# Ranks zero and one of a mixture of experts leave by 32-wide turns on VectorE, rank one gets a narrow arm, and two late ranks hold 248 and 240 tokens

## The chip, the core and the metric

One NeuronCore of one Trainium2 chip runs the whole program in one launch. The metric is the device time of that launch in microseconds (us), the median of three runs. Beside it stands one profiled execution, from which every duration below is read.

## What is computed

The input is attention data (8 batches, 8 heads, 576 positions, 64 wide). Two attentions are added: one over means of four positions, spread back, and one over a band of seven neighbours. The result, laid out as 4608 tokens of 512 numbers, goes through a two-level mixture of 4 x 4 experts, and that part is what the change touches:

```python
g_idx = argmax(x @ w_group); e_idx = argmax(x[g] @ w_expert[g])   # one of 16 experts a token
h = np.maximum(xg[mask_e] @ w1[g, e], 0.0)        # 512 -> 1024
ye = h @ w2[g, e]                                 # 1024 -> 512
out[tok_idx] = (g_w * e_w)[:, None] * ye          # the token's own two softmax weights
```

All is float32. With the reference's own inputs (its routing, evaluated on them) one expert, with 329 tokens, is taken early; the other fifteen have 385, 366, 360, 312, 305, 300, 281, 265, 261, 260, 258, 246, 237, 233 and 210 tokens.

## The kernel before, in words

The attention comes first, with one expert (256 of its tokens early, the rest late) worked in beside its end. The other fifteen experts follow in order of size as ranks 0 to 14. An order written out by hand covers the attention; `begin` is a written list of steps that finishes the early expert and prepares rank 0; `main` then emits `ranked` for ranks 0 to 13, and `last_rank` does rank 14. Each engine executes its own instructions strictly in the order in which they were emitted.

A rank has a fixed width, `CAPS[r]`, in tokens. Each product of a pair of float32 operands is three TensorE matmuls (high by high, high by low, low by high). `hidden` makes one of eight 128-row blocks of h: 12 matmuls as wide as the rank. `project` adds one block into the result: 12 matmuls as wide as the rank (four 128-row parts of the result, tokens along the columns), or, where the width is a multiple of 128, three matmuls of 512 columns for each 128 tokens (tokens along the rows; "rows" in the code). So ranks 1, 13 and 14 (384, 256, 256) were projected by rows before.

`ranked` runs ten steps f. At f = 0 it drains the previous rank's result out of PSUM, GpSimd fetches the tokens of the rank after next by indirect DMAs, and from f = 2 on `project(f - 2)` writes the same PSUM banks again. Within the ten steps VectorE and ScalarE also split the next weights into high and low, and prepare the next rank's tokens.

A result leaves in one of three ways. Ranks 2 to 12 (`TURNED`): VectorE turns 32 x 32 blocks straight out of PSUM (`drain`), and GpSimd scatters 32 tokens at a time in quarter rows (`store_quarters`, up to 13 scatters); the columns of `w2` are permuted on the host for this (`w2q`), and the tokens' weights are multiplied in on the way in (`scale`, ScalarE, 128 x 512 for each 128 tokens). Rank 0: two copies on ScalarE and two on VectorE out of PSUM, then for each 128 tokens four TensorE transposes, a multiplication by the weight on ScalarE or VectorE (`store`) and one scatter of whole rows. Rank 1, 13, 14, by rows: `store` alone.

The tokens of ranks 0 and 1 are turned by TensorE on their way in (`turn_in`), those of later ranks by a DMA to and from DRAM (`lay_down`, `pick_up`) and VectorE.

Ranks in `SWITCHED` (0 and 3 to 12) exist twice, once at full width and once narrower by `LESS` = 20. A word of bits, computed from the counts, decides by a branch on every engine; the narrow arm is the one jumped to. TensorE gets a prefetch hint for the branch at f = 2 of the rank before. All eleven branches took the narrow arm here.

Seven steps of `begin`, in their order (late is the early expert's rest, st is rank 0):

```python
(self.weights_split, st, 0, "w2", V),
(self.weights_in, st, e, 2),
(self.project, late, 2),
(self.project, late, 3),
(self.turn_in, st, 0),
(self.turn_in, st, 1),
(self.turn_hidden, late, 3),
```

## Time and profile before

| | |
|---|---|
| three runs | 682.92, 684.72, 686.47 us; median 684.72 us |
| the profiled execution | 685.44 us; its span in the trace 683.7 us |
| TensorE matmul busy | 642.7 us (94% of the span) |
| VectorE, ScalarE, GpSimd busy | 489.3, 384.5, 353.7 us |
| DMA | 160.77 MB, mean 235 GB/s |

"Busy" counts the time in which at least one instruction of the engine runs. Matmuls overlap and their ends are modelled, so the distance between their starts says more than their durations. Lines such as L979 are lines of the kernel before: L979 and L995 hidden, L1028 and L1030 project (by rows, by columns), L964 `turn_in`, L1058 the transposes of `store`, L931 `scale`, L1041 `drain` by turns, L1072 the scatters, L1178 the branches, L886 the high half of a weight split, L957 that of tokens.

### The profile page before, as it was taken

How to read it: one execution, taken by the hardware profiler on the slowest of the kernel's cores; microseconds unless marked ns; L12 is line 12 of the kernel's file. 1: busy time of each engine (PE TensorE's matmuls, PEld its weight loads, DVE VectorE, ACT ScalarE, POOL GpSimd, SP SyncE). 2: the span in 40 equal slices, each digit the busy share in tenths (PEclk: the TensorE clock that was granted, in tenths of full speed). 3: DMA queues.
4: the chain of work that ended last, by engine and by line, in shares of the span. 5: the costliest groups of instructions: out<-in, count | busy, mean ns of one | idle time of the engine just before them, and what ended most of it. 6: DMA issues, size and time to landing. Idle time of an engine off the chain costs nothing. (4 is left out here: it accounts for less than half of the span.)

```text
span 683.7 us, 17694 instructions
## 1 busy us (share of the span) xinstructions
PE 642.7 (94%) x6743; PEld 573.8 (84%) x6743; DVE 489.3 (72%) x942; ACT 384.5 (56%) x833; POOL 353.7 (52%) x394
## 2 busy tenths in 40 slices
PE   7788997998987899999999999999999999999996
PEld 3565776676765788999899999999999999999995
DVE  5987988988896587644646667776776776777751
ACT  8776765775764536645544446456456456456531
POOL 7957556667542553403240446557547556455521
PEclk9999999999999999999999999999999999999999
DMA  8788899889778618959786778989999989999920
GB/s 305 207 253 264 270 295 269 272 230 263 238 207 263 201 29 265 319 166 247 222 218 203 206 217 235 250 264 280 234 271 277 253 250 273 270 271 268 284 70 27
DMA packets 128080, 160.77 MB, mean 235 GB/s; under 512 B 25445, under 2 KB 92783, under 8 KB 127968
## 3 DMA queue, kind: packets, MB, share of 16 engines
q1 hardware_dynamic: 102496, 129.99, 65.7%
q0 software_dynamic: 7952, 20.47, 10.1%
q10 hardware_dynamic: 17520, 8.85, 4.8%
q8 instruction: 66, 1.08, 0.7%
q14 instruction: 46, 0.38, 0.2%
HBM read 129.48 MB, written 31.03 MB: 235 GB/s over the span
## 5 line engine op out<-in xcount | busy, mean ns | idle before, releaser
L1072 POOL DMA_INDIRECT out_dram<-yt,qo x110 | 130.2, 1184 | 133.2 <-DVE qo L831 107.9
L983 ACT ACTIVATE hh<-ph 128x256 fp32r<-128x256 f32 (+13 forms) x128 | 53.3, 418 | 185.9 <-PE ph L979 184.0
L979 PE MATMUL ph<-xh,w1h 128*128 128x256 f32 (+13 forms) x512 | 153.8, 301 | 2.9 <-issue 2.8
L979 PE MATMUL ph<-xh,w1l 128*128 128x256 f32 (+13 forms) x512 | 153.0, 299 | 0.5 <-issue 0.5
L979 PE MATMUL ph<-xl,w1h 128*128 128x256 f32 (+13 forms) x512 | 153.1, 299 | 0.0
L984 DVE SCALAR_TENSOR_TENSOR hl<-ph,hh 128x256 fp32r<-128x256 f32 (+13 forms) x128 | 59.1, 464 | 86.4 <-ACT hh L983 86.0
L1030 PE MATMUL y<-hh,w2h 128*128 128x396 f32 (+11 forms) x384 | 115.9, 302 | 0.0
L1030 PE MATMUL y<-hh,w2l 128*128 128x396 f32 (+11 forms) x384 | 115.2, 300 | 0.5 <-issue 0.5
L1030 PE MATMUL y<-hl,w2h 128*128 128x396 f32 (+11 forms) x384 | 115.2, 300 | 0.0
L979 PEld LDWEIGHTS ph<-xh,w1h 128*128 128x128 f32 x512 | 96.6, 189 | 4.9 <-issue 4.0
L979 PEld LDWEIGHTS ph<-xl,w1h 128*128 128x128 f32 x512 | 96.7, 189 | 0.9
L979 PEld LDWEIGHTS ph<-xh,w1l 128*128 128x128 f32 x512 | 96.6, 189 | 0.1
L887 DVE TENSOR_TENSOR w2l<-raww,w2h 128x1024 fp32r<-128x1024 f32 x61 | 74.6, 1223 | 26.8 <-ACT w2h L886 24.8
L887 DVE TENSOR_TENSOR w1l<-raww,w1h 128x1024 fp32r<-128x1024 f32 x61 | 74.6, 1224 | 23.4 <-ACT w1h L886 22.6
L914 POOL DMA_INDIRECT xg<-xd,gi x47 | 53.2, 1132 | 54.9 <-ACT share L927 25.9
L1030 PEld LDWEIGHTS y<-hh,w2h 128*128 128x128 f32 x384 | 72.3, 188 | 1.3 <-ACT w2h L886 0.7
L1030 PEld LDWEIGHTS y<-hh,w2l 128*128 128x128 f32 x384 | 72.3, 188 | 0.7 <-issue 0.7
L1030 PEld LDWEIGHTS y<-hl,w2h 128*128 128x128 f32 x384 | 72.3, 188 | 0.0
L886 ACT ACTIVATE w1h<-raww 128x1024 fp32r<-128x1024 f32 x64 | 67.3, 1053 | 6.1 <-PE phr L995 2.7
L886 ACT ACTIVATE w2h<-raww 128x1024 fp32r<-128x1024 f32 x64 | 67.1, 1050 | 1.0 <-DMA raww<-in_moe_w_dram 1.0
L1072 POOL DMA_INDIRECT out_dram<-yo,oi x14 | 15.9, 1134 | 53.5 <-ACT yo L1063 20.6
L452 PE MATMUL b_x<-vw,pt 126*32 126x128 f32 x1152 | 38.0, 275 | 3.9 <-DMA vw<-odd 2.4
(247 smaller groups left out, 1268.3 us busy)
## 6 DMA issues: line engine op xcount, KB each, us to landing
raww<-in_w1q_dram SPq DMA_DIRECT2D x52, 512.0 KB
raww<-in_w2q_dram SPq DMA_DIRECT2D x44, 512.0 KB
raww<-in_moe_w_dram SPq DMA_DIRECT2D x32, 512.0 KB
vw<-in_vw_dram SPq DMA_DIRECT2D x32, 378.0 KB
kt<-in_k_dram SPq DMA_DIRECT2D x16, 576.0 KB
qT<-in_q_dram SPq DMA_DIRECT2D x16, 576.0 KB
xd<-x ACTq DMA_DIRECT2D x15, 576.0 KB
vs<-in_vm_dram SPq DMA_DIRECT2D x16, 512.0 KB
```

Source lines behind the costliest of these rows:

```text
L452: self.nc.tensor.matmul(pt[32 * j : 32 * j + 32, t], self.of("pt", u)[:ROWS, 32 * lin : 32 * lin + 32], self.windows(u)[:ROWS, :, lin], st ...
L886: self.nc.scalar.activation(hi, raw, AF.Copy)
L887: eng.tensor_tensor(out=lo, in0=raw, in1=hi.bitcast(F32), op=ALU.subtract)
L914: self.nc.gpsimd.indirect_dma_start(out=xg[:w], out_offset=None, in_=self.xd[0:rows], in_offset=bass.IndirectOffsetOnAxis(ap=st["gi"][:w, ...
L979: nc.tensor.matmul(ph, a[:, k, cs], st[b][:, k, 0:C], start=(n == 0), stop=(n == 11))
L983: nc.scalar.activation(hh, ph, AF.Relu)
L984: nc.vector.scalar_tensor_tensor(out=hl, in0=ph, scalar=0.0, in1=hh.bitcast(F32), op0=ALU.max, op1=ALU.subtract)
L1030: nc.tensor.matmul(y, a[:, f % 2, cs], b, start=(f == 0 and n == 0), stop=(f == 7 and n == 2))
L1072: i = self.nc.gpsimd.indirect_dma_start(out=out, out_offset=bass.IndirectOffsetOnAxis(ap=index, axis=0), in_=y, in_offset=None, bounds_che ...
```

## The change

Rank 0 and rank 1 join `TURNED`: their results leave by VectorE's turns and quarter scatters, their `w2` is read permuted, and their tokens are scaled on the way in, rank 0's by four steps in `begin` ahead of `turn_in`, rank 1's at f = 2, 3, 4 of rank 0 (rank 2's then at 4, 5, 6, and its `lay_down` at 7). Rank 1 joins `SWITCHED` with arms of 384 and 368 columns, and is projected by columns. Ranks 13 and 14 get 248 and 240 columns; they stay by rows. The lists of quarter rows have four columns for 13 ranks, the quarter's number is added when they are made, and the matrix they are made with lies in a result buffer. The copies, the transposes in `store`, and `keep_shares` for ranks go. Cut to its core:

```diff
-CAPS = [416, 384, 368, 352, 336, 320, 312, 304, 296, 288, 280, 272, 264, 256, 256, 384]
-LESS = 20
-SWITCHED = (0, *range(3, 13))
-TURNED = range(2, 13)
+CAPS = [416, 384, 368, 352, 336, 320, 312, 304, 296, 288, 280, 272, 264, 248, 240, 384]
+LESS = [16 if r == 1 else 20 for r in range(16)]
+SWITCHED = (0, 1, *range(3, 13))
+TURNED = range(13)
-SCALED = {3: (0,), 4: (1,), 5: (2,)}
...
     def quarter_lists(self, c):
-        pt = self.psum([P, hi - lo, 3], "ql")
...
-        self.nc.vector.tensor_copy(self.qf[:, c], pt)
+        pt = self.psum([P, hi - lo, 4], "ql")
...
+        self.nc.vector.tensor_scalar(out=self.qf[:, c], in0=pt, scalar1=self.quad, scalar2=None, op0=ALU.add)
...
+        self.four = self.yt[1][:, 0 : 4 * P].rearrange("p (c q i) -> p c q i", c=4, q=4)
...
     def drain(self, st):
-        for d in range(4):
-            if d % 2:
-                nc.vector.tensor_copy(yt[:, d], st["y"][d])
-            else:
-                nc.scalar.activation(yt[:, d], st["y"][d], AF.Copy)
+        nb = (st["C"] + 31) // 32
+        yt = st["yt"] = self.yt[st["r"] % 2][:, 0 : P * nb].rearrange("p (b d j) -> p b d j", d=4, j=32)
         for d in range(4):
+            self.nc.vector.transpose(yt[:, :, d], self.ys[d][:, 0 : 32 * nb].rearrange("p (b i) -> p b i", i=32))
...
     def store(self, st, t):
-            y = self.psum([P, DM], "yr")
-            for d in range(4):
-                nc.tensor.transpose(y[:m, P * d : P * d + P], st["yt"][:, d, c : c + m], self.idf)
...
+    def rows(self, st):
+        return st.get("r", NE) not in TURNED
...
             (self.project, late, 3),
+            *((self.scale, st, t) for t in range(len(st["xg"]))),
             (self.turn_in, st, 0),
...
-                if st["r"] < 2:
-                    self.keep_shares(st)
...
-                    for t in range(3):
+                    for t in range(4):
                         self.store_quarters(pv, 4 * t + SCATTER.index(f))
...
-            for t in SCALED.get(f, ()):
-                if nn and t < len(nn["xg"]):
-                    self.scale(nn, t)
+            for x, lo in ((nx, 2 if first else 10), (nn, 4 if first else 3)):
+                if x and 0 <= f - lo < len(x["xg"]):
+                    self.scale(x, f - lo)
...
-            if nn and f == 6:
+            if nn and f == 6 + first:
                 self.lay_down(nn)
```

## Rows read from the trace of the kernel before

**Rows 1.** The page's busy times of the whole span.

```profile
PE 642.7 (94%) x6743; PEld 573.8 (84%) x6743; DVE 489.3 (72%) x942; ACT 384.5 (56%) x833; POOL 353.7 (52%) x394
```

**Rows 2.** TensorE's waits from 250 us on: waiter <- releaser: total us, times, longest.

```profile
PE ph L979 <- issue: 3.4, 4, 1.3
PE y L1030 <- issue: 0.5, 1, 0.5
```

**Rows 3.** Timeline, TensorE: first matmul of ranks 1, 2, 3 (start, duration in us).

```profile
309.19 0.34 PE L979 MATMUL ph<-xh,w1h 128*128 128x384 f32 x1
...
344.48 0.33 PE L979 MATMUL ph<-xh,w1h 128*128 128x368 f32 x1
...
377.32 0.32 PE L979 MATMUL ph<-xh,w1h 128*128 128x332 f32 x1
```

**Rows 4.** TensorE's groups in rank 1: the transposes of rank 0's results (busy, mean ns).

```profile
L1058 PE MATMUL yr<-idf,yt 128*128 128x128 f32 x12 | 1.8, 272 | 0.0
L1058 PE MATMUL yr<-idf,yt 128*32 128x128 f32 x4 | 0.6, 272 | 0.0
```

**Rows 5.** Who waited for y (344 to 353 us): us, times.

```profile
  PEld y L1030: 0.5, 2
```

**Rows 6.** Timeline, VectorE, where rank 2 ends: its drain and the next high-low split.

```profile
375.96 2.14 DVE L1041 STREAM_TRANSPOSE yt<-y 128x384 f32<-128x384 f32 x4 [1.04 <-PE y L1030]
379.91 0.50 DVE L984 SCALAR_TENSOR_TENSOR hl<-ph,hh 128x332 fp32r<-128x332 f32 x1 [1.81 <-ACT hh L983]
```

**Rows 7.** The page's group of quarter scatters (busy, mean ns, idle before).

```profile
L1072 POOL DMA_INDIRECT out_dram<-yt,qo x110 | 130.2, 1184 | 133.2 <-DVE qo L831 107.9
```

**Rows 8.** Timeline, TensorE: matmuls 1 and 13 of hidden in ranks 12 and 13.

```profile
610.62 0.28 PE L979 MATMUL ph<-xh,w1h 128*128 128x244 f32 x1
...
611.98 0.28 PE L979 MATMUL ph<-xh,w1h 128*128 128x244 f32 x1
...
633.19 0.28 PE L979 MATMUL ph<-xh,w1h 128*128 128x256 f32 x1
...
634.60 0.28 PE L979 MATMUL ph<-xh,w1h 128*128 128x256 f32 x1
```

**Rows 9.** Timeline, ScalarE, in `begin`, around rank 0's first token splits.

```profile
266.69 1.06 ACT L886 ACTIVATE w2h<-raww 128x1024 fp32r<-128x1024 f32 x1
267.64 0.93 ACT L957 ACTIVATE xh<-xt 128x416 fp32r<-128x416 f32 x2
268.44 0.41 ACT L957 ACTIVATE hrh<-ht 128x256 fp32r<-128x256 f32 x1
```

**Rows 10.** Timeline, TensorE, the same stretch: `turn_in` of rank 0, then `turn_hidden`.

```profile
266.63 1.32 PE L964 MATMUL xt<-idf,xg 128*128 128x128 f32 x8
267.88 0.44 PE L1003 MATMUL ht<-idf,hr 128*128 128x128 f32 x2
```

**Rows 11.** Timeline, ScalarE, in rank 0: one `scale` and the instruction behind it.

```profile
288.52 0.71 ACT L931 ACTIVATE xg<-xg 128x512 f32<-128x512 f32 x1
289.14 1.05 ACT L886 ACTIVATE w1h<-raww 128x1024 fp32r<-128x1024 f32 x1
```

**Rows 12.** Windows: length, PE, PEld, DVE, ACT, POOL busy, granted clock, DMA share, GB/s.

```profile
225.50:227.70 2.20, 0.04 (x1) 0.00 (x0) 0.56 (x1) 0.92 (x3) 1.97 (x1) 0.95 0.56 188
227.70:231.00 3.30, 3.29 (x16) 3.30 (x17) 1.45 (x3) 1.75 (x4) 1.96 (x1) 0.51 0.64 184
```

**Rows 13.** TensorE's branches: into ranks 3 to 7, then 8 to 12 (ns min/median/max).

```profile
L1178 PEldq COMPARE_BRANCH  x5: 328/328/352, 374.5 to 484.5; - x5
...
L1178 PEldq COMPARE_BRANCH  x5: 1605/2535/3323, 509.9 to 608.7; - x5
```

**Rows 14.** Timeline, TensorE: the last matmuls of rank 8, the first of rank 9.

```profile
536.59 0.29 PE L1030 MATMUL y<-hl,w2h 128*128 128x276 f32 x1
536.72 0.28 PE L1030 MATMUL y<-hh,w2l 128*128 128x276 f32 x1
538.15 0.39 PE L979 MATMUL ph<-xh,w1h 128*128 128x268 f32 x1 [1.15 <-issue]
```

**Rows 15.** The page's queue of instruction DMAs: packets, MB, share of 16 engines.

```profile
q8 instruction: 66, 1.08, 0.7%
```

## The prediction

> **What bounds the kernel now.** First the busy times: TensorE computes for 94% of the span, VectorE for 72%, ScalarE for 56% [rows 1]. Then TensorE's waits in the part that the change touches, from 250 us on: 3.9 us in some 430, all of them put to "issue", that is, to no other engine and no DMA [rows 2]. So through the ranks a microsecond off another engine is worth nothing unless TensorE waits for it, and a matmul less is worth its whole length. Then the starts of the ranks, since starts are exact where durations are modelled: rank 1 lasts from 309.19 to 344.48, 35.29 us, and rank 2, with 368 columns, from 344.48 to 377.32, 32.84 us [rows 3]. The reader should see in these three views a queue of matmuls that rarely runs dry: the change is a sum of matmuls taken out, plus every place where it makes TensorE stop.

> **Rank 1, by columns and narrow.** The counts (366 tokens, and 368 is the narrow arm's edge) put rank 1 in its narrow arm. It then does what rank 2 does: 192 matmuls of 368 columns, no transposes, a result drained by turns. Rank 2's 32.84 us hold one wait that rank 1 will not have: matmuls of y waited 0.5 us for the last `store` of rank 1 [rows 5], and a drain by turns is over before `project` asks. So rank 1 should take 32.3 to 32.8 us and give back 2.5 to 3.0; I take 2.9. As a check by parts: of 35.29 us the sixteen transposes of rank 0's results are 2.4 us of modelled busy time [rows 4], overlapped, so less in starts; and 16 columns less out of 384, over both halves, is 4% of the rest, 1.4 us. Both ways lie near each other. The 0.5 us that rank 2 lost comes back too: rank 1's result no longer leaves by `store`. **Sum so far: -3.4 us.**

> **The work that takes their place.** The four turns of a 384-wide result took 2.14 us on VectorE, and the next split, which stands behind them in VectorE's queue, still waited 1.81 us for ScalarE after them [rows 6]. At 416 columns in rank 1 they are about 2.3 us. `project` writes these banks only after 24 hidden matmuls, about 4 us later (24 of 192, of 32.84 us). They are covered; without that cover they would cost 2.3 us a rank. GpSimd gets 13 and 12 scatters of 1.18 us for 4 and 3 [rows 7], 17 us in a rank of 32, behind the three fetches of the rank after next, which it issues first; it idled 133 us in front of the quarter scatters, so nothing waits. The bytes scattered are the same. The lists' four matmuls become 19 columns wider: under 0.1 us. The wider `quarter_list` and the moved `quad` are single VectorE instructions of 0.2 us that replace others. Rank 1's three scales and rank 2's later ones are ScalarE work of 0.6 us each beside matmuls, on an engine that idles 44% of the time [rows 1]; `lay_down` moves one step later, and its reader stands in the next rank. I put all of these at nothing, with a bound of +0.5.

> **Ranks 13 and 14.** 12 hidden matmuls take 1.41 us at 256 columns and 1.36 at 244 [rows 8], 0.05 us for 12 columns. Eight columns less in 96 matmuls give 0.27 us, sixteen give 0.53: **-0.8 us**. The projections keep their 512 columns. Nothing in these rows suggests a step below 256 columns: 244 is simply a little cheaper. Both counts (233 and 210) fit, so the overflow loop stays closed.

> **What `begin` pays.** Here I expect the loss. The four scales of rank 0 stand on ScalarE behind the weight split at 266.69 and before the token splits, so they start at 267.64 [rows 9]. One lasts 0.71 us, and the next instruction starts 0.62 after it [rows 11]; four end at 267.64 + 3 x 0.62 + 0.71 = 270.2. TensorE began `turn_in` at 266.63 and came to the next step at 267.88 [rows 10]. Now the fourth transpose of the first block must wait for the fourth scale, until 270.2; it and the second block's four take another 0.75, so the next step starts at 271.0. That is **+3.1 us** with nothing to hide it: the projections and rank 0's first matmuls queue behind these transposes on the one in-order engine. The lower bound is nothing (if ScalarE came early: it has no slack just there, the rows are back to back); the upper bound is 3.5, with 0.1 us for each hand-over.

> [...] The new stop is 1.7 us without any matmul, then single transposes 0.6 apart. [...]

> **The new branch, and where the branches lie.** This is the term that no row settles. TensorE's own branch took 0.33 to 0.35 us going into ranks 3 to 7, and 1.6 to 3.3 us going into ranks 8 to 12 [rows 13]. A short one hides behind matmuls already queued. A long one doesn't always: going into rank 9 the starts are 1.43 us apart where 0.13 is usual [rows 14], so 1.3 us were lost, with 3.32 - 1.3 = 2.0 us covered, which is sixteen matmuls of 0.127. Five such places, three at a branch and two inside ranks 10 and 12, make the 3.9 us of issue waits; with 0.16 each that the modelled end hides (1.31 for 1.15) they are 4.7 us. Instruction DMAs fetch 1.08 MB in 66 packets, 16 KB each [rows 15], and the late ranks differ from the early ones in width but not in instructions, so a long branch looks like one whose target had not been fetched. The change puts a second copy of rank 1 ahead of all of them, so every later branch falls elsewhere among those 16 KB pieces. Bounds: if all the late ones became short, -4.7 us; if all five early ones and rank 1's took 3.32 us, each would lose 3.32 less the cover of sixteen matmuls at its own spacing (0.127 at 276 columns, 32.84 / 192 = 0.171 at 368, and in line with these elsewhere: 2.9 us after rank 0, 2.2 after rank 6), which is 0.4 + 0.6 + 0.9 + 1.0 + 1.1 + 1.2 = +5.2. Between these I take **-1.2**: the bad state may move either way, but it costs less where matmuls are wide, and ranks 1 to 7 are the wide ones.

> **The sum** on the profiled execution (685.44 us; its span is 683.7, with 1.7 around it): -3.4 - 0.8 + 3.1 + 1.6 - 1.2 = -0.7, so 684.7. That execution lies 0.7 above the median of the runs, 684.72, so I predict **684.0 us**.

> **Rivals.**

> *The stop in `begin` does not open.* Then the gain stands alone: 684.72 - 4.2 - 1.2 = 679.3. For it: rank 0's tokens had landed, since TensorE took them without a gap at 266.63. Against it: ScalarE's queue, which is where the scales stand, was full to 268.4 [rows 9]. Chance 0.08.

> *The stop opens, but the late branches become short.* 684.72 - 4.2 + 4.7 - 4.7 = 680.5. For it: five branches of 0.33 us show what is possible at the same size of code [rows 13]. Against it: they may be long because the matmuls are short there, and then nothing changes. Chance 0.19. Both of these are faster by more than 0.5%, which is 3.4 us and about what a measurement of this kernel can tell from no change.

> *The early branches become long.* With every one at 3.32 us: 684.72 + 0.5 + 5.2 = 690.4, slower. It decides from +2.9 us on, that is, if more than half of that happens while the late ones stay long. For it: one place in the code moves them all, and a new one is added. Against it: wide matmuls cover most of a long branch. Chance 0.07. [...]

> *The change does what it says and nothing shows*: this is my forecast, chance 0.66, between 681.5 and 686.8 by itself: the clock spared (-1.6), the scales cheaper or dearer by half a microsecond, the branches 2 us either way.

> So faster 0.27, same 0.66, slower 0.07. The range goes from 680.0, which leaves out about one in ten at the fast end, to 686.8, about as many above it.

> **What would show each step.** Rank 0 should begin 3 to 5 us later for what `begin` loses, and rank 1 last 32.3 to 32.8 us from first matmul to first matmul; rank 2 should last 32.4. The page should hold no transposes in `store`. In `begin` ScalarE should show four scales directly behind the weight split of w2, TensorE a gap of 1.7 us in front of `turn_in`, waiting for ScalarE, and the granted clock should fall right after it. VectorE's four turns in rank 1 should end more than a microsecond before the first `project`. TensorE's branch into rank 1 should be visible, with its length, and the branches into 8 to 12 should tell which rival holds: if they are 0.33 us and the waits for issue are gone, I am too slow by 3 to 4 us. The prediction is wrong in its mechanism if TensorE does not stop before `turn_in`, if matmuls of y wait for the turns at f = 2, or if GpSimd's scatters hold back a fetch so that `turn_in` or the token splits come late.

## The result and the profile after

The changed kernel takes 676.92 us (median of six runs, 673.91 to 678.90); the kernel before, beside it, 683.82 us. The ratio is 0.9876, 95% interval 0.9838 to 0.9913: 1.2% faster, below the forecast of 684.0 us and below its range. On four later occasions the changed kernel, timed again beside the one before, came to ratios of 0.9898 to 0.9908 (table below), so the gain is 6 to 8 us.

First the page's busy times, its group of quarter scatters and its queue of instruction DMAs, which answer to [rows 1, 7, 15]:

```profile
PE 638.7 (95%) x6751; PEld 573.1 (85%) x6751; DVE 487.3 (72%) x954; ACT 385.0 (57%) x831; POOL 370.2 (55%) x428
...
q8 instruction: 62, 1.02, 0.6%
...
L1051 POOL DMA_INDIRECT out_dram<-yt,qo x135 | 156.6, 1160 | 135.1 <-DVE qo L832 102.8
```

TensorE lost 4 us of busy time and 8.3 us of span. (1.4 us of the span lie ahead of `begin`, in attention, which the change leaves alone.) So much of what was gained had been idle time, not work. GpSimd's 25 new scatters changed nothing: it still idles 135 us in front of them.

TensorE's waits from 250 us on, against [rows 2] (waiter <- releaser: total us, times, longest):

```profile
PE xt L960 <- ACT xg L927: 2.5, 4, 1.6
PE xt L960 <- DMA xg<-xd,gi: 0.8, 1, 0.8
PE y L1024 <- DVE hrl L954: 0.3, 1, 0.3
PE ph L975 <- PE y L1024: 0.2, 1, 0.2
```

The 3.9 us of waits for issue are gone, all of them. In their place stands the new stop of `begin`, `turn_in` (L960) waiting for ScalarE's `scale` (L927). The branches tell why. This is the line of the branches, TensorE's row, ranks 1 and 3 to 12 (ns min/median/max), for [rows 13]:

```profile
L1161 PEldq COMPARE_BRANCH  x11: 328/328/352, 308.3 to 602.3; - x11
```

Not one is long. Then the starts (timeline, TensorE, first matmuls of ranks 0, 1, 2, 3, 13, 14), for [rows 3, 8]:

```profile
273.99 0.45 PE L975 MATMUL ph<-xh,w1h 128*128 128x396 f32 x1 [0.18 <-PE y L1024]
...
311.09 0.34 PE L975 MATMUL ph<-xh,w1h 128*128 128x368 f32 x1
...
343.32 0.33 PE L975 MATMUL ph<-xh,w1h 128*128 128x368 f32 x1
...
375.58 0.32 PE L975 MATMUL ph<-xh,w1h 128*128 128x332 f32 x1
...
625.53 0.28 PE L975 MATMUL ph<-xh,w1h 128*128 128x248 f32 x1
...
646.31 0.27 PE L975 MATMUL ph<-xh,w1h 128*128 128x240 f32 x1
```

Rank 1 lasts 32.23 us and rank 2 32.26, together 3.64 less than the 68.13 of [rows 3]. From rank 3 to rank 13, where TensorE has the same work as before, it is 249.95 us where it was 255.87 (377.32 in [rows 3] to 633.19 in [rows 8]): **5.9 us less in ranks whose matmuls the change doesn't touch**.

Last `begin`, ScalarE and then TensorE (timelines, for [rows 9, 10]):

```profile
264.86 1.06 ACT L885 ACTIVATE w2h<-raww 128x1024 fp32r<-128x1024 f32 x1
265.81 2.54 ACT L927 ACTIVATE xg<-xg 128x512 f32<-128x512 f32 x4
```

```profile
266.58 0.33 PE L960 MATMUL xt<-idf,xg 128*128 128x128 f32 x1 [1.64 <-ACT xg L927]
267.19 0.33 PE L960 MATMUL xt<-idf,xg 128*128 128x128 f32 x1 [0.28 <-ACT xg L927]
...
269.23 0.44 PE L999 MATMUL ht<-idf,hr 128*128 128x128 f32 x2
```

The four scales stand directly behind the split of w2 and TensorE stops 1.64 us for the first of them, as forecast. The windows on both sides of the fourth transpose (length, then busy times, granted clock, DMA share, GB/s), for [rows 12]:

```profile
264.95:268.40 3.45, 0.99 (x3) 0.42 (x3) 2.23 (x3) 3.40 (x6) 0.16 (x1) 1.00 0.66 216
268.40:271.80 3.40, 3.40 (x20) 2.64 (x20) 1.88 (x4) 2.59 (x5) 0.00 (x0) 1.00 0.59 180
```

In this execution the clock stayed at 1.00 behind the stop. VectorE's turns behave as those of [rows 6]: in rank 1 the four turns of rank 0's result take 2.10 us and the next split still waits 1.68 us for ScalarE; of rank 1's result, in rank 2, it is 2.08 and 2.02 us.

### The profile page after: what moved, and what is told of

Its sections match the earlier page's. It is cut to its first block, busy times and chain, and to the rows that moved or that the text cites. A ratio compares the mean times of both kernels' runs of the same rounds, so it can differ in the third digit from the quotient of the medians.

```text
span 675.4 us, 17805 instructions
## 1 busy us (share of the span) xinstructions
PE 638.7 (95%) x6751; PEld 573.1 (85%) x6751; DVE 487.3 (72%) x954; ACT 385.0 (57%) x831; POOL 370.2 (55%) x428
## 3 DMA queue, kind: packets, MB, share of 16 engines
q8 instruction: 62, 1.02, 0.6%
## 5 line engine op out<-in xcount | busy, mean ns | idle before, releaser
L1051 POOL DMA_INDIRECT out_dram<-yt,qo x135 | 156.6, 1160 | 135.1 <-DVE qo L832 102.8
L979 ACT ACTIVATE hh<-ph 128x368 fp32r<-128x368 f32 (+14 forms) x128 | 52.8, 415 | 176.0 <-PE ph L975 174.7
L975 PE MATMUL ph<-xh,w1h 128*128 128x368 f32 (+14 forms) x512 | 152.7, 299 | 0.2 <-PE y L1024 0.2
L975 PE MATMUL ph<-xh,w1l 128*128 128x368 f32 (+14 forms) x512 | 152.3, 298 | 0.0
L975 PE MATMUL ph<-xl,w1h 128*128 128x368 f32 (+14 forms) x512 | 152.3, 298 | 0.0
L1026 PE MATMUL y<-hh,w2h 128*128 128x368 f32 (+11 forms) x416 | 126.2, 303 | 0.0
L1026 PE MATMUL y<-hl,w2h 128*128 128x368 f32 (+11 forms) x416 | 125.8, 302 | 0.0
L1026 PE MATMUL y<-hh,w2l 128*128 128x368 f32 (+11 forms) x416 | 125.7, 302 | 0.0
L980 DVE SCALAR_TENSOR_TENSOR hl<-ph,hh 128x368 fp32r<-128x368 f32 (+14 forms) x128 | 58.7, 461 | 75.4 <-ACT hh L979 74.9
L954 DVE TENSOR_TENSOR xl<-xt,xh 128x256 fp32r<-128x256 f32 (+16 forms) x68 | 30.4, 450 | 16.3 <-ACT xh L953 16.1
```

The costliest lines, as they stand in the source:

```text
L954: self.nc.vector.tensor_tensor(out=lo, in0=x, in1=hi.bitcast(F32), op=ALU.subtract)
L975: nc.tensor.matmul(ph, a[:, k, cs], st[b][:, k, 0:C], start=(n == 0), stop=(n == 11))
L979: nc.scalar.activation(hh, ph, AF.Relu)
L980: nc.vector.scalar_tensor_tensor(out=hl, in0=ph, scalar=0.0, in1=hh.bitcast(F32), op0=ALU.max, op1=ALU.subtract)
L1026: nc.tensor.matmul(y, a[:, f % 2, cs], b, start=(f == 0 and n == 0), stop=(f == 7 and n == 2))
L1051: i = self.nc.gpsimd.indirect_dma_start(out=out, out_offset=bass.IndirectOffsetOnAxis(ap=index, axis=0), in_=y, in_offset=None, bounds_che ...
```

## The experiments

**The theory.** The instruction DMAs fetch pieces of 16 KB [rows 15]. From 12 to 205 us TensorE of the kernel before executed 3239 matmuls and 3239 weight loads while 26 such packets came, 249 for each packet, its semaphore instructions not counted; from this a piece is put at 256 instructions, an estimate. Counted in these steps, a branch into a rank stands at some place from 0 to 255 of its piece. A switched rank's two arms are 783 instructions, three pieces and 15, so the place moves on by 15 from one rank to the next. In the kernel before the branches into ranks 3 to 7 stand at 145, 160, 175, 190 and 205 and are short; those into 8 to 12 stand at 220, 235, 250, 9 and 24 and are long. The change moves all of them by 168: 57 to 192, with rank 1's at 172. So a branch would be long when it stands near the end of a piece or at the start of the next. (Its target, some 390 instructions on, and its prefetch hint move along with it, so "the place of a branch" here means the place of all three; no run moves them apart.) **The rivals**: late ranks have long branches because their matmuls are short; any displacement or longer program changes them; or the gain is that of the narrower ranks and the branches are a by-product.

All pads below are one edit with another count N: N matmuls, each with its weight load, so 2N instructions, in rank 0's other arm, which never executes. (Where an expectation speaks of 58, 132, 142, 168, 224 or 256 matmuls of this kind, these are instructions.) Each group of the table is one occasion, on which its kernels ran beside the kernel before.

```diff
         ph = self.psum([P, C], "ph")
+        for _ in range(N if f == 0 and st.get("r") == 0 and "arm" not in st else 0):
+            nc.tensor.matmul(ph, wh[:, 0, cs], st["xh"][:, 0, 0:C], start=True, stop=True)
```

| kernel | ratio to before | interval | branches over 1 us into ranks 1 to 12 | rank 3 to rank 13, us |
|---|---|---|---|---|
| *before at 690.37 us* | | | | |
| before, N = 84 (before_moved) | 0.9935 | 0.9908 to 0.9962 | none | 256.42 |
| after, N = 44 (after_moved_back) | 0.9948 | 0.9917 to 0.9979 | 8, 9, 10, 11, 12 | 257.01 |
| after, no scale in begin | 0.9828 | 0.9783 to 0.9872 | none | 255.31 |
| after, scales on two engines | 0.9850 | 0.980 to 0.990 | none | 253.49 |
| *before at 690.63 us* | | | | |
| after (after_again) | 0.9908 | 0.9873 to 0.9942 | none | 251.76 |
| after, N = 128 (after_moved_whole) | 0.9877 | 0.9829 to 0.9924 | none | 252.04 |
| after, N = 29 (after_moved_part) | 0.9954 | 0.9923 to 0.9984 | 11, 12 | 254.10 |
| after, rank 1 at 384 | 0.9906 | 0.9869 to 0.9943 | none | 252.30 |
| *before at 691.40 us* | | | | |
| after (after_third) | 0.9898 | 0.9854 to 0.9943 | none | 253.82 |
| after, fill in begin | 0.9856 | 0.9802 to 0.9911 | none | 252.47 |
| after, N = 66 (after_moved_early) | 0.9968 | 0.9935 to 1.0001 | 5, 6, 7 | 252.20 |
| after, ranks 13, 14 at 256 | 0.9896 | 0.9864 to 0.9928 | none | 253.48 |
| *before at 684.55 us* | | | | |
| after (after_fourth) | 0.9903 | 0.9878 to 0.9929 | none | 249.94 |
| after, early fill in begin | 0.9884 | 0.9859 to 0.9909 | none | 249.94 |
| before (before_again), one execution | | | 8, 9, 10, 11, 12 | 260.89 |
| after, N = 66 (moved_early_again), one execution | | | 5, 6, 7, 8 | 253.66 |
| *before at 683.87 us* | | | | |
| before, N = 84 (before_moved_again) | 0.9926 | 0.9892 to 0.9959 | none | 250.28 |
| after (after_fifth) | 0.9908 | 0.9873 to 0.9943 | none | 249.94 |

**The branches moved in the kernel before.** N = 84, 168 instructions.

> The kernel before, with 84 matmuls that are never executed put into rank 0's wide arm, so that every later branch lies 168 instructions further on, where the changed kernel has it within its 16 KB pieces. No executed instruction differs. Theory (where a branch lies decides whether it is long): the branches into ranks 8 to 12 fall from 1.6 to 3.3 us to 0.33, the waits for issue go, and the time falls by 4 to 5 us, from about 683.8 to 679. Rival (the late branches are long because the ranks are narrow or the DMA queues full there): nothing changes, 683.8, and the same five branches stay long.

All ten branches became short and the kernel gained 0.65%, 4.5 us. But its profile still lost 6.1 us against the 250.28 of the last rows of the table, in short stops that the branches don't explain (TensorE's waits from 280 us on):

```profile
PE y L1032 <- DVE hl L986: 1.9, 3, 0.9
PE y L1032 <- issue: 0.4, 1, 0.4
PE ph L981 <- issue: 0.4, 1, 0.4
```

Such stops, in other late ranks each time, show in most profiles of the occasions on which the kernel before took 690 to 691 us, and in none of the changed kernel on the others. On the same occasions ScalarE's first split of rank 0's w1 in `begin` started 14.1 to 14.3 us after the DMA of its weights was issued, where it is 11.1 to 11.4 us on the others, for both kernels alike (but for after_spread, which moves that split). The stops blur the single profiles of those occasions.

**The branches moved back in the changed kernel.** N = 44: ranks 3 to 12 stand again at 145 to 24.

> The changed kernel, with 44 matmuls that are never executed in rank 0's wide arm, so that the branches into ranks 3 to 12 lie within their 16 KB pieces where the kernel before had them. Theory: the branches into ranks 8 to 12 become long again (1.6 to 3.3 us), the one into rank 1 too, but wide matmuls cover it; the time rises by 4 to 5 us from 676.9 to about 681.5. Rival: 676.9, all branches at 0.33 us.

TensorE's branch rows, up to rank 7 and from rank 8:

```profile
L1163 PEldq COMPARE_BRANCH  x6: 328/338/433, 310.9 to 485.3; - x6
...
L1163 PEldq COMPARE_BRANCH  x5: 1785/3392/3645, 510.8 to 609.9; - x5
```

The five long ones are back in the same ranks, and so are 5.8 us of waits for issue. The ratio of 0.9948 is 0.7% above that of the changed kernel in the first result, but on another occasion; beside the displaced kernel before (0.9935) it is hardly slower, and the two profiles, 256.42 and 257.01 us from rank 3 to 13, don't separate them either.

**The changed kernel beside a displacement by a whole piece and one that moves three.**

> The changed kernel itself, as the yardstick for the three that run beside it. Both theories: 1.2% faster than the kernel before (ratio 0.984 to 0.991), every branch of TensorE that leads into a rank 0.33 to 0.35 us, no wait for issue in the ranks.

> The changed kernel with 256 matmuls (16 KB of TensorE's program) that never execute, in rank 0's other arm, so that every later branch stands 16 KB further on, at the same place of its piece. By the place in the piece (my theory): no change, ratio to the changed kernel 0.998 to 1.002, all branches 0.33 to 0.35 us. By the other reading, that any longer program or any displacement brings the long branches back: ratio to the changed kernel 1.005 or more, with branches of 1.6 us and over.

> The changed kernel with 58 matmuls that never execute in rank 0's other arm. Counted in TensorE's program in pieces of 256 instructions, the branches into ranks 10, 11 and 12 then stand at 220, 235 and 250, as those into ranks 8, 9 and 10 did in the kernel before, the one into rank 1 at 230, and those into ranks 3 to 9 at 115 to 205. My theory: long branches (1.6 to 3.7 us) into ranks 10, 11, 12 and 1, short ones (0.33 to 0.35) into 3 to 9, and 2 to 3.5 us more than the changed kernel (ratio 1.003 to 1.005). The rival, that late ranks have long branches because their matmuls are short or because the program is long ahead of them: long ones into ranks 8 and 9 too, or none.

The displacement by 256 instructions changes nothing (ratio 0.9877 beside 0.9908, no long branch), so neither a longer program nor a displacement as such matters. The part makes branches long in late ranks alone that stand late in their piece (rows up to rank 10, and ranks 11 and 12; then the starts of ranks 11 and 12):

```profile
L1163 PEldq COMPARE_BRANCH  x9: 328/328/429, 312.3 to 560.8; - x9
...
L1163 PEldq COMPARE_BRANCH  x2: 3627/3658/3688, 583.8 to 608.1; - x2
```

```profile
587.53 0.39 PE L977 MATMUL ph<-xh,w1h 128*128 128x252 f32 x1 [1.58 <-issue]
...
611.87 0.38 PE L977 MATMUL ph<-xh,w1h 128*128 128x244 f32 x1 [1.69 <-issue]
```

Two of four came true: 235 and 250 are long; 220, into rank 10, took 0.33 us here, and 230, into rank 1, 0.43. Ranks 8 and 9, long in the kernel before, are short. Ranks 10 and 11 last 24.75 and 24.34 us, 1.7 and 2.0 more than the 23.01 and 22.38 that they take without a long branch (after_fourth). The prediction's cover of sixteen matmuls gives 3.63 - 16 x 0.120 = 1.7 and 3.69 - 16 x 0.117 = 1.8. The ratio is 0.46% above that of the changed kernel beside it, as expected, though the intervals overlap.

**The long branches moved into early ranks.** N = 66: 219, 234, 249, 8 and 23 for ranks 5 to 9.

> The changed kernel with 132 matmuls that never execute in rank 0's other arm. By TensorE's program in pieces of 256 instructions the branches into ranks 6, 7, 8 and 9 then stand at 234, 249, 8 and 23, the one into rank 5 at 219, at the edge, those into ranks 3 and 4 at 189 and 204, into 10, 11 and 12 at 38, 53 and 68, into 1 at 48. My theory, the place in the piece: long branches (1.6 to 3.7 us) into 6 to 9, which are early ones of 0.33 us in both kernels, perhaps into 5 and 10, short ones elsewhere; 1.5 to 3.5 us more than the changed kernel, less than the five late ones cost, since sixteen matmuls cover 2.1 to 2.3 us at 284 to 292 columns. The rival, that only late ranks can have long branches: all short, or long ones into 8 to 12 alone.

> The kernel whose branches into ranks 6 to 9 stand at 234, 249, 8 and 23, profiled a second time, because the execution profiled first was the fastest of its twelve and showed long branches into 5, 6 and 7 alone. By the place in the piece the long ones are there again, and in 8 and 9 in some executions. If the lengths are a matter of chance and not of place, long ones appear into other ranks this time, 3 and 4 or 11 and 12 among them.

Both profiles have long branches into 5, 6 and 7, the second into 8 too; its rows, ranks 1 to 4, 5 to 8 and 9 to 12:

```profile
L1163 PEldq COMPARE_BRANCH  x3: 328/351/352, 308.8 to 402.7; - x3
...
L1163 PEldq COMPARE_BRANCH  x4: 1860/2279/3275, 430.7 to 509.6; - x4
...
L1163 PEldq COMPARE_BRANCH  x4: 338/355/425, 534.7 to 605.3; - x4
```

Ranks 5 to 7 had 0.33 to 0.34 us in every other kernel, so it isn't the ranks; it is the place. Over all kernels, branches at 234 to 250 that led into ranks 3 to 12 were long, in every profile; at 219 and 220 five of six, at 8 and 9 four of five, at 23 and 24 three of five. So the edges are a matter of the single execution. The first of these profiles was the fastest of its twelve executions (681.7 us, median 687.6); timed, the kernel has a ratio 0.7% above that of the changed kernel beside it, more than the 1.5 to 3.5 us expected. The second took 681.4, 4.0 more than the median of the changed kernel beside it, and 3.7 more from rank 3 to 13 than after_fourth: 1.0 in rank 4 (3.28 us into rank 5, 0.96 by the cover), 0.5 in rank 7, and 2.0 in ranks 11 and 12, in stops for issue without a long branch:

```profile
587.10 0.28 PE L977 MATMUL ph<-xl,w1h 128*128 128x252 f32 x1 [1.08 <-issue]
...
609.60 0.38 PE L977 MATMUL ph<-xh,w1h 128*128 128x244 f32 x1 [0.55 <-issue]
```

Counted in the program as the branches were, these two matmuls stand at 228 and 232 of their pieces. The five other stops for issue of over 0.25 us inside ranks 3 to 12 of the kernels with long branches (two in the kernel before, in ranks 10 and 12, and one each in before_again, after_moved_back and after_moved_early) stand at 223, 228, 223, 228 and 232. By these counts TensorE was stopped in the last part of a piece where no branch stands too (seven times, for 0.5 to 1.5 us), and the stops moved along with the branches.

**The kernel before once more.**

> The kernel before on this chip, for its profile. My theory of the prediction's begin term: its begin lasts 42.8 to 46.4 us (the first as profiled before the prediction, the second as with the branches moved), so the change costs begin 4 us and more here, not 3.1. Branches of 1.6 to 3.7 us into ranks 8 to 12, 0.33 to 0.35 into 3 to 7. If the gain comes from the branches' place, ranks 7 to 12 together last 4 to 6 us longer than in the changed kernel beside it.

```profile
L1178 PEldq COMPARE_BRANCH  x5: 328/328/352, 371.4 to 481.5; - x5
...
L1178 PEldq COMPARE_BRANCH  x5: 2345/3274/4352, 506.9 to 610.5; - x5
```

```profile
511.31 0.46 PE L979 MATMUL ph<-xh,w1h 128*128 128x276 f32 x1 [2.11 <-issue]
```

```profile
511.50:514.90 3.40, 3.40 (x16) 3.40 (x16) 0.07 (x1) 0.50 (x2) 1.98 (x3) 0.50 1.10 247
```

The same five are long, up to 4.35 us. Behind one stop, of 2.11 us, TensorE's clock was 0.50 for 3.4 us (last row). From rank 3 to 13 this execution took 260.89 us, 10.9 more than the changed kernel. Its `begin`, counted from the first hidden matmul of the early tokens' second part to rank 0, lasts 42.3 us; in the changed kernel beside it (after_fourth) 47.1, 4.9 us more, so the expected 4 us and more came true here.

**The gain divided.** The two kernels with short branches, side by side.

> The kernel before with 168 matmuls that never execute in rank 0's other arm, so that its branches stand where the changed kernel's do, nothing else changed, a second time, now beside the changed kernel on one chip. My theory, that the branches' place alone gives most of the gain: ratio to the kernel before 0.989 to 0.994, all branches 0.33 to 0.35 us, ranks 7 to 12 together 4 us or more shorter than with long branches. The rival, that the narrower rank 1 and ranks 13 and 14 give it: ratio 0.998 or more.

> The changed kernel beside the one before it in this list, both with short branches: what is left between the two is the rest of the change, by the sum's measured terms -3.6 for ranks 1 and 2, -0.7 for 13 and 14, +3.1 for begin and 0 to +3.4 for the clock behind the stop, -1.2 to +2.2 us together, a ratio of the two of 0.998 to 1.003. The rival, that the rest gives as much as the branches: a ratio of the two of 0.995 or less.

The kernel before, only its branches moved (ranks 0, 1, 3, 13 and 14, after the start from which `begin` is counted):

```profile
225.98 0.37 PE L981 MATMUL ph<-xh,w1h 128*128 128x256 f32 x1
...
268.58 0.45 PE L981 MATMUL ph<-xh,w1h 128*128 128x396 f32 x1 [0.29 <-PE y L1030]
...
305.61 0.34 PE L981 MATMUL ph<-xh,w1h 128*128 128x384 f32 x1
...
373.74 0.32 PE L981 MATMUL ph<-xh,w1h 128*128 128x332 f32 x1
...
624.02 0.28 PE L981 MATMUL ph<-xh,w1h 128*128 128x256 f32 x1
...
645.10 0.28 PE L981 MATMUL ph<-xh,w1h 128*128 128x256 f32 x1
```

The changed kernel:

```profile
224.12 0.36 PE L975 MATMUL ph<-xh,w1h 128*128 128x256 f32 x1
...
269.65 0.35 PE L975 MATMUL ph<-xh,w1h 128*128 128x396 f32 x1
...
306.65 0.34 PE L975 MATMUL ph<-xh,w1h 128*128 128x368 f32 x1
...
371.14 0.31 PE L975 MATMUL ph<-xh,w1h 128*128 128x332 f32 x1
...
621.08 0.28 PE L975 MATMUL ph<-xh,w1h 128*128 128x248 f32 x1
...
641.86 0.27 PE L975 MATMUL ph<-xh,w1h 128*128 128x240 f32 x1
```

Moving the branches alone gives 0.74%, 5.1 us, inside the expected 0.989 to 0.994; from rank 3 to 13 it is 250.28 us for the 255.87 of the kernel before, 5.6 less. The rest of the change gives 0.2% by the two ratios (0.9926 to 0.9908), 1.2 us, which the intervals don't tell from nothing, and which is inside the expected 0.998 to 1.003. Stage by stage from the two lists: `begin` 42.60 to 45.53, +2.9; rank 0 no change; ranks 1 and 2 68.13 to 64.49, -3.6; ranks 3 to 12 250.28 to 249.94, -0.3; rank 13 -0.3, rank 14 to the end of the span (674.6, 671.0) -0.4. Together -1.7. So some four fifths of the gain is the place of the code, by the ratios (0.74 of 0.92%) and by the starts (5.6 of 7.3 us), which the diff says nothing about. The share is not sharp: on the first occasion the place alone gave 0.65%, and the rest of the change with the long branches kept (after_moved_back) 0.52%, each with an interval of some 0.3% either way.

**What the scales in `begin` cost.** Left out (rank 0's tokens then go in unweighted), and shared between ScalarE and VectorE ahead of the weight splits:

```diff
-            *((self.scale, st, t) for t in range(len(st["xg"]))),
```

> The changed kernel without the four scales of rank 0 in begin: rank 0's tokens are left without their weights, all else is the same, and later branches move by four instructions only. Theory (the stop of TensorE before turn_in is a pure loss): the gap of 1.6 us and the three small ones go, rank 0 starts 3.1 to 3.3 us earlier, time about 673.7. Rival (the stop only shifts a wait that comes anyway, for weights or tokens): rank 0 becomes longer by as much and the time stays at 676.9.

> The changed kernel with rank 0's scales ahead of the weight splits of chunk 0 in begin, two on ScalarE and two on VectorE, and those weight splits behind the first token splits. Theory: the last scale ends about 1 us after TensorE is ready instead of 3.3, the stop shrinks to under 1 us, time 674 to 674.7. Rival: the weight splits now come late and rank 0's first hidden matmuls wait for them, so that the time stays at 676.9 or rises.

Without them the ratio is 0.9828, the lowest of all, and `begin` lasts 44.9 us where 50.3 to 50.9 was usual on occasions like it. The gain over the changed kernel, 0.5 to 0.8% by its ratios elsewhere, was not timed side by side. Sharing them gave a ratio that can't be told from no change, and the stop didn't shrink to under 1 us as expected; `begin` lasts 48.0 us. TensorE still stopped 2.7 us, because ScalarE itself came late to the step ahead of the scales, and the clock fell for 6.8 us (matmuls of `project` 0.43 us apart there, 0.23 ahead of the stop).

**What the clock costs behind the stop.** The changed kernel was profiled five times. Three times the stop ahead of `turn_in` was 1.63 to 1.64 us; of these the result's profile and after_fifth kept the clock, and after_fourth didn't. (moved_early_again, whose `begin` is the same, kept it too: a stop of 1.63 us, 45.5 us in all.) Twice it was 4.4 to 4.6 us, when ScalarE began the split of w1 some 2.9 us later, on the occasions on which the kernel before took 690 us; what held that split there isn't settled.

> The changed kernel itself again, as the yardstick for the three beside it: ratio to the kernel before 0.985 to 0.993. Its profile is looked at in begin: the stop ahead of turn_in was 1.64 us with the clock kept at 1.0 in the profile of the result, and 4.4 to 4.5 us with the clock at 0.5 for 6.8 us behind it in four later ones. If the length of the stop is a matter of the single execution, either may be seen here; if of the chip, one of them throughout.

> The changed kernel itself, as the yardstick for the fill beside it: ratio to the kernel before 0.985 to 0.993, the stop ahead of turn_in 4.4 to 4.6 us with the clock at 0.5 behind it if this chip does as the two chips before it did, begin 50.3 to 50.9 us from the first hidden matmul of the early tokens' second part to rank 0.

In after_fourth, whose stop and gaps are the same to 0.01 us, the clock falls 0.9 us after the start of the fourth transpose; the stretch at the lower level, and one as long ahead of it:

```profile
262.00:265.45 3.45, 1.91 (x9) 1.09 (x10) 1.39 (x3) 2.99 (x6) 0.00 (x0) 1.00 0.78 235
265.45:268.86 3.41, 3.41 (x11) 2.67 (x11) 2.52 (x4) 1.96 (x3) 0.00 (x0) 0.50 0.37 127
```

The matmuls of `project` start 0.42 to 0.43 us apart there and 0.23 to 0.24 in the result's profile. `begin` takes 47.1 us here, 45.9 and 45.5 in the two that kept the clock: the clock costs 1.3 to 1.6 us. Behind a stop of 4.4 us or more, which six displaced or altered kernels had too, it fell every time, for 6.8 us or longer (0.50 for 6.80 us in after_again, for 6.83 in after_third). To see whether the clock is what such a stop costs, sixteen useless matmuls were put into it (with N = 112, so that fill and pad are one whole piece):

```diff
             (self.project, late, 3),
+            (self.fill, late, 3),
...
+    def fill(self, st, f):
+        y = self.psum([P, DM], "ht")
+        for _ in range(16):
+            self.nc.tensor.matmul(y, st["h", f][0], st["w2", f // 2][0][:, f % 2], start=True, stop=True, skip_group_check=True)
```

> The changed kernel with sixteen matmuls of 512 columns (some 3.8 us at full clock) put on TensorE between the last project and turn_in in begin, writing a bank that nobody reads, and 224 that never execute in rank 0's other arm, so that the later branches stand at the same places. My theory, that the stop is paid twice, as idle time and by the clock that falls behind it: where the stop is 4.4 us, what is left of it is 0.7 us, the clock stays at 1.0 and rank 0 starts 3 to 3.4 us earlier, ratio to the changed kernel 0.995; where the stop is 1.6 us, the fill is 2.1 us too long and the ratio is 1.003. The rival, that the clock falls by the transposes that stand 0.6 us apart and not by the stop: the clock is 0.5 there all the same and nothing is gained.

> The changed kernel with the sixteen useless matmuls again, but on tokens turned one step earlier, so that they don't wait for ScalarE and start right behind the last project. My theory: no idle time of more than 1 us ahead of turn_in, the clock at 1.0 throughout, begin 47 to 47.6 us long where the changed kernel's is 50.3 to 50.9 (the 3.4 us that the lower clock takes), and a ratio to the changed kernel of 0.995. The rival, that the end of begin is set by ScalarE and VectorE and not by TensorE's clock: begin is no shorter than the 49.2 us of the first fill.

The first fill used block 5, which ScalarE turns late, so it waited 2.98 us itself; still the clock stayed at 1.00 and `begin` took 49.2 us for 50.7 beside it (after_third), 1.5 us less where 3 to 3.4 were expected. The second, on block 3, started at once and left no stop:

```profile
265.00:268.50 3.50, 3.50 (x17) 2.82 (x16) 2.72 (x3) 3.50 (x7) 1.01 (x1) 1.00 0.52 175
268.50:275.28 6.78, 6.78 (x37) 5.08 (x35) 3.74 (x6) 5.25 (x9) 0.00 (x0) 1.00 0.46 148
```

`begin` took 46.0 us, 1.1 less than in after_fourth with 3.9 us of matmuls added, but no less than the 45.5 to 45.9 of the three executions that kept the clock by themselves. Each of these is a single execution. The expected 47 to 47.6 us was for a stop of 4.4 us, which this occasion didn't have. Both fills have a lower ratio than the changed kernel beside them (0.9856 for 0.9898, 0.9884 for 0.9903), and the intervals overlap both times. If they are better than the changed kernel, it is by 0.2 to 0.4%.

**The widths.** Rank 1 with one arm (`SWITCHED` without 1, and N = 71 to keep the branches in place), and ranks 13 and 14 at 256:

> The changed kernel with one arm alone for rank 1, which so takes all 384 columns for its 366 tokens; 142 matmuls that never execute keep the later branches where they stand. The sum's check by parts: the sixteen columns are 4% of what rank 1 works, so it lasts 1.3 to 1.4 us longer (33.5 to 33.7 us from start to start), rank 2 as long as before, and the whole 1.0 to 1.4 us more than the changed kernel, since a branch of 0.35 us goes away. The rival, that a rank's length is set by the spacing of instructions and not by columns (nothing below 400 columns): rank 1 stays at 32.2 us.

> The changed kernel with ranks 13 and 14 at 256 columns as before; every branch stands where it stood. By the sum both ranks together are 0.7 to 0.8 us longer from start to start, 0.24 to 0.3 in rank 13 and 0.36 to 0.53 in rank 14, and nothing else changes: ratio to the changed kernel 1.001, which the timing can't tell from 1. The rival, a step of the matmul below 256 columns, would show 2 us or more.

Starts of ranks 1 and 2 in the first, of 13 and 14 in the second:

```profile
314.05 0.34 PE L977 MATMUL ph<-xh,w1h 128*128 128x384 f32 x1
...
347.58 0.33 PE L977 MATMUL ph<-xh,w1h 128*128 128x368 f32 x1
```

```profile
633.86 0.28 PE L975 MATMUL ph<-xh,w1h 128*128 128x256 f32 x1
...
654.99 0.28 PE L975 MATMUL ph<-xh,w1h 128*128 128x256 f32 x1
```

Rank 1 at 384 lasts 33.53 us, 1.3 more than at 368: of the 3.06 us that rank 1 gave back, 1.3 are columns, and the other 1.8 are left for the transposes, the drain by copies and the projection by rows, which no run takes apart. Rank 13 at 256 lasts 21.13 us, 0.35 more than at 248, a little above the expected 0.24 to 0.3, and rank 14, to the end of the span, 0.4 more than at 240. There is no step between 240 and 256 columns.

## Why the prediction was wrong

The step that failed is the branches' term, "-1.2" in the sum. It should have been -5.6: by place all five late branches became short, and none of the early ones long. Of the 7.1 us between 684.0 and 676.92 that is 4.4; the clock's +1.6, of which the result's profile shows nothing (whether the executions that weren't profiled kept the clock isn't known), would be 1.6 more, the kernel before, that much faster beside it, 0.9, and ranks 1 and 2 are 0.2. The end that the text had as its bound for this case, -4.7, was itself too small by about 1 us, because it priced only the gaps that the waits list, with 0.16 us added to each. By starts, against the changed kernel, rank 8 alone lost 1.4 us and ranks 7 and 9 to 12 another 4.4. The text saw the displacement ("every later branch falls elsewhere among those 16 KB pieces") and then took it as a coin to toss, though the place of a branch can be counted: two arms of a rank are a fixed number of instructions. What happened is the second rival, "the stop opens, but the late branches become short", at 0.19; its 680.5 us was 3.6 too slow, by the last three of these and 0.9 for the branches.

The other terms held. Ranks 1 and 2: -3.4 forecast, -3.6 measured, and "32.3 to 32.8" for rank 1 became 32.2. Ranks 13 and 14: -0.8 forecast, -0.7 measured. The stop in `begin`: +3.1 forecast, +2.9 to +3.1 measured where the clock was kept, in the place, with the length (1.64 for 1.7) and by the engine that the text named. On the fourth occasion, with the clock lost, it is +4.9, about the sum's 3.1 and 1.6 together; on the first, where the kernel before (before_moved) stopped 1.76 us there itself, 46.4 to 50.6, +4.2. The clock: +1.6 forecast, half of the 3.30 us at 0.51 in [rows 12], behind a stop of 2.2 us; no run ahead of the forecast shows it for a stop of 1.7 us. The runs showed nothing in the result's profile, 1.3 to 1.6 in after_fourth, and 6.8 us at 0.50 on the occasions when the stop was 4.4 us; the size is right for a short stop, but whether it falls due differs from one execution to the next. With sixteen matmuls put there it stayed at 1.00, in both kernels. That three executions with the same stop of 1.63 to 1.64 us kept the clock and one lost it shows that the length of the stop alone doesn't tell whether it happens.

The turns, the scatters, the lists and the scales of later ranks, taken at nothing, cost nothing: the waits name none of them, and rank 0 lasts 37.0 us in both kernels with short branches. One reading was incomplete: [rows 2] leave out a wait of 0.7 us for a DMA, at 252.4 us, so not all waits from 250 us on were for issue. The changed kernel has that wait too (0.8 us), so the sum doesn't change by it.

The third rival, long early branches, didn't come true in this change, but N = 66 shows that it can: another length of rank 1's second copy would have brought long ones into ranks 5 to 8. The instruction DMAs fetch pieces of the same size after the change (62 packets, 1.02 MB), and the runs agree that the place within such a piece decides. Being taken doesn't make a branch long: all branches here were taken, and those into ranks 1 and 3 to 12 at 57 to 205 took 0.33 to 0.35 us in every profile. Nor does the number of pieces up to the target, some 390 instructions on, sort them: by count it lies in the next piece for branches at 57 to 117, which were short, and for those at 9 and 24, which were mostly long, and one piece further both for those at 130 to 205, which were short, and for those at 219 to 250, which were mostly long. All of them had a prefetch hint.

What stays open: why a branch near a piece's edge takes 1.6 us once and 4.4 another time; why rank 1's branch at 230 and at 4 took only 0.43 us, and rank 0's, at 67 to 103, between 0.5 and 3.0 us in every kernel; whether the place that counts is the branch's own, its target's or its hint's; and what makes the late ScalarE in `begin` and the short stops in late ranks on the occasions of 690 us. (Those put to issue stand at 37 to 204 of their pieces, so they aren't the ones at the edges.)

## What to carry to other kernels

Code that is added or removed ahead of a chain of branches moves every branch behind it among the pieces in which instructions are fetched, and that can be worth more than the work that was edited (some 5 to 6 us of 6 to 8 here). Before a change is credited, compare the stretches that it doesn't touch, start to start; if they changed too, move the branches of the kernel before by code that never executes and time that. And time put ahead of TensorE's next step in a stage without slack was paid in full here (a stop of 1.64 us and three gaps of 0.28 made `begin` 2.9 to 3.1 us longer), and in one execution of four paid again by the clock (1.3 to 1.6 us).

## What the runs showed of the hardware

Behind the same stop of 1.64 us with the same three gaps of 0.28 TensorE's clock was 0.50 for 3.4 us in one execution (after_fourth) and 1.00 in three others. Behind a wait at a branch it was 0.50 too: 2.11 us without a matmul, then 3.4 us at 0.50 (before_again).

Matmuls whose result nobody reads, put into a stop, cost next to nothing: with 3.9 us of them the clock stayed at 1.00 and `begin` took 46.0 us, for 47.1 in an execution without them that lost the clock and 45.5 to 45.9 in three that kept it.
